# One queue's transfers laid out as landing in order, more zero groups, twelve pattern buffers in reused space

## The chip, the cores and the metric

The kernel runs on one core of a Trainium2 chip. The metric is the device time of one execution in microseconds (us). TensorE (PE) multiplies matrices into the eight PSUM banks; VectorE (DVE), ScalarE (ACT) and GpSimd (POOL) compute; SyncE (SP) issues almost all DMA transfers of this kernel, on one queue. Every engine runs its own instruction list in order and waits on semaphores for the others.

## The reference

One transformer layer in its parallel form, batch 1, 2048 rows of width 640, bf16: an attention with 32 query heads of 20 columns that share one key and one value head, and a feed-forward part with a squared ReLU (640 to 1536 to 640). Both read the same normalised input and both are added to it:

```python
def _A_ref(x, wq, wk, wv, wo):
    q = (x @ wq).reshape(B, S, 32, 20).transpose(0, 2, 1, 3)
    k = x @ wk
    v = x @ wv
    scores = jnp.einsum("bhqd,bkd->bhqk", q, k) * (20 ** -0.5)
    p = softmax(scores)
    o = jnp.einsum("bhqk,bkd->bhqd", p, v)
    return o.transpose(0, 2, 1, 3).reshape(B, S, 640) @ wo

def _B_ref(x, w1, b1, w2, b2):
    h = x @ w1 + b1
    r = jnp.where(h > 0, h, 0)
    return (r * r) @ w2 + b2

xn = layernorm(x)
out = x + _A_ref(xn, ...) + _B_ref(xn, ...)
```

## The kernel before, in words

**Tiling.** Queries come in 4 chunks of 512 rows, heads in 8 groups of four; a chunk and a group are a *block*, 32 in all, worked off in order. Within a block the keys come in 16 tiles of 128. One *unit* is one head of one key tile: a score matmul of 128 keys by 512 queries that fills one PSUM bank. There are 32 x 16 x 4 = 2048 units; up to four score matmuls use the four row strips of the array at once and count as one batch.

**Two ways to the exponential.** ACT takes two or three neighbouring banks in one instruction and writes exp into the ring `PT` (L1328). To relieve ACT, some key tiles (all four heads of one) go another way: DVE turns scores into 16-bit integer patterns that, read as bf16, are a piecewise-linear power of two (L1425, one bank each), and from these 2048 columns it makes three shifted copies (L1446); part of the third copies is made by POOL in pieces (L1508). The four patterns are averaged with weighted values `vp` by the value product. Patterns lie in `pbx`, `NPB` buffers of four banks' width. [...]

**Value product and norm.** The value product (L1615) sums a block into one PSUM bank; a column of ones in the values gives the softmax's denominator. `norm(b)` then copies the bank to `Tn` (L1660, DVE), spreads the denominator over the partitions by a DMA (L1663, `dn`), takes the reciprocal (L1665, DVE), sends it to a row by a second DMA (L1668, `Rr`), spreads it by a third (L1671, `Rb`, 256 KB), and POOL multiplies (L1676). Four DMAs (L1721) then pack the result into `OTp`. The last three blocks use `norm_last`: DVE transposes, reciprocal, multiply into `T2`, transpose back (L1696 to L1708).

**The rest.** Query projections (`u_QP`: PE, DVE L888, and 20-row DMAs L906 into `qT`), the feed-forward part (`u_FFN`: PE L777, DVE L933, POOL L941) and the output products are *units of filler work* for PE between the score batches, each tied to a position in blocks (`U(at, ...)`). For the last chunk, the output rows 12 to 15 (of 128 each) are split: `u_P1` does feed-forward and the attention parts that are ready, and puts the sum into `part` with the residual (L1055); `u_PF` adds the remaining head tiles after the last block; `u_PX` does one row (NPX = 1) in one go, residual included through an identity matmul. The residual `xres` is loaded again row by row (`x_again`, L952), in four buffers.

**What sets the order.** A planner in Python, run when the kernel is built. It holds a duration for every instruction and a landing time for every DMA, keeps a clock for each engine, and picks the next instruction by earliest start and priority. The result is one fixed list per engine; the semaphores are derived from it. On the chip the lists run as laid out, whatever the real durations. `PLAN` holds thresholds for each half block (how early scores are issued ahead of ACT, `lead`; how much work DVE should have waiting, `hungw`, `dstarv`; how many banks are kept for filler, `miscr`; and so on). `dma(eng, name, fn, deps, land, issue)` lays a transfer out as occupying its queue for `issue` ns and landing `land` ns after its start. `S_FILL` adds groups of four matmuls with zero weights (L1544) that change nothing in the sums, where PE's load over the last `PE_FWIN` = 1500 ns, in columns, is not over a limit: `PE_FILL` up to position `FILLPOS` = 4 blocks, `PE_FILL2` behind it.

Of the kernel before, what the change touches and what calls it, by code (L numbers as in the profile page):

```python
# [14 lines left out]
HPG = 4  # L15
# [35 lines left out]
NPB = 10  # L51
PHQ = 2
PHP_F, PHP_E = 156.0, 0.836
OVER = 40.0
PHU = 5000.0
NQS = 6
NQP = 2
EVP = 2
# [93 lines left out]
)]  # L152
PAAT = 24.7
PAQ = ()
NPX = 1
PQAT = (7.0, 10.5)
PQSTEP = .3
XRP = 2.0
PASTEP = .12
TLAND = 3050.0  # L160
TDMA = 4
NLAST = 3
NTN = 3
DAL, DBL, DCL, NBL, QSL, XRL = 2800.0, 2400.0, 7600.0, 2300.0, 2700.0, 3600.0
CLTL = 9000.0
PVEND = 0.5
PTOL = 500.0
# [1752 lines left out]
```

## Time and profile before

| | us |
|---|---|
| median of three runs | 703.27 (703.08 to 704.89) |
| the profiled execution | 703.88 |
| its span, first to last instruction | 702.2 |
| busy: PE / DVE / ACT / POOL | 684.5 / 669.6 / 675.8 / 415.4 |

The granted TensorE clock is 0.993 of full speed in the mean. PE's busy time counts matmuls that overlap, so it says little of how full PE is. In lines of the profile, `out<-in` names the tiles written and read, `x8` a count of instructions, and what stands in brackets is the engine's idle time before the line and who ended it; `SPq` is the DMA-issuing queue of SP, `issue` a wait for nothing that the profile shows.

### The profile page before, as it was taken

The numbers are of one execution on the slowest core, as the hardware profiler recorded it, in microseconds if no ns is written. First come the engines' busy times: TensorE is split into PE (matmuls) and PEld (weight loads), VectorE is DVE, ScalarE is ACT, GpSimd is POOL, SyncE is SP. The second block draws the span as 40 slices with busy tenths as digits, with TensorE's granted clock in tenths as the row PEclk, the third lists the DMA queues.
The fourth block names the chain that finished last, engine by engine and source line by source line (L and its number), as shares of the span: only waits on it lengthen the run. The fifth ranks groups of instructions, "written<-read, shape, count | busy, mean of one in ns | idle before, by whom it ended". The sixth has DMA issues, their size and how long they took to land.

```text
span 702.2 us, 23386 instructions
## 1 busy us (share of the span) xinstructions
PE 684.5 (97%) x9882; PEld 220.0 (31%) x9882; DVE 669.6 (95%) x1161; ACT 675.8 (96%) x696; POOL 415.4 (59%) x687
## 2 busy tenths in 40 slices
PE   8899899899999999999999999999999999999997
PEld 4322222222223333332222333333222233333335
DVE  7988899999999999999999999999999999999983
ACT  6999799999999999999999999999999999999993
POOL 2256476676764666667666666666776666645500
PEclk9999899999999999999999999999999999999999
DMA  7722222111100111111110121010110101112001
GB/s 209 181 50 66 71 76 66 25 22 29 27 17 10 37 27 44 38 29 33 28 27 16 25 50 41 17 43 18 44 30 18 23 17 33 42 34 52 21 2 40
DMA packets 38658, 29.46 MB, mean 42 GB/s; under 512 B 20922, under 2 KB 34203, under 8 KB 38555
## 3 DMA queue, kind: packets, MB, share of 16 engines
q1 hardware_dynamic: 37899, 27.95, 16.7%
q8 instruction: 79, 1.29, 0.8%
q14 instruction: 24, 0.20, 0.1%
q10 hardware_dynamic: 656, 0.03, 0.1%
HBM read 10.87 MB, written 2.62 MB: 19 GB/s over the span
## 4 chain that ended last, share of the span: by engine, by line
PE 48%; DVE 30%; ACT 16%; DMA 4%; issue 1%; SPq 1%; POOL 1%; DVEq 0%; POOLq 0%
PE ps L1615 17%; ACT PT L1328 16%; DVE pbx L1425 16%; PE ps L1148 15%; PE ps L777 15%; DVE pbx L1446 8%; DVE hT_tmp L933 2%; DMA Rb<-Rr 1%; DVE Tn L1660 1%; DMA dn<-Tn 1%; SPq L906 1%; DVE qpk L888 1%; DMA xnT<-big 1%; DVE stats L679 1%; DMA pbx<-in_A_x_dram 0%
## 5 line engine op out<-in xcount | busy, mean ns | idle before, releaser
L1328 ACT ACTIVATE PT<-ps 128x1024 bf16<-128x1024 f32 (+1 forms) x678 | 668.8, 1119 | 9.1 <-PE ps L1148 8.4
L1508 POOL TENSOR_SCALAR pbx<-pbx 128x576 int16<-128x576 uint16 (+15 forms) x509 | 311.5, 634 | 163.7 <-DVE pbx L1446 161.5
L1425 DVE TENSOR_SCALAR pbx<-ps 128x512 int16<-128x512 f32 (+1 forms) x583 | 381.7, 684 | 10.2 <-PE ps L1148 9.3
L1148 PE MATMUL ps<-qT,kT 20*128 20x512 bf16 x2048 | 265.6, 386 | 6.1 <-DVE hT_tmp L933 2.5
L1446 DVE TENSOR_SCALAR pbx<-pbx 128x2048 int16<-128x2048 int16 x313 | 214.4, 707 | 0.5
L1615 PE MATMUL ps<-pbx,vp 128*32 128x512 bf16 x1776 | 164.8, 387 | 2.7 <-DVE pbx L1446 1.4
L1148 PEld LDWEIGHTS ps<-qT,kT 20*128 20x128 bf16 x2048 | 66.3, 91 | 263.1 <-ACT PT L1328 159.9
L1615 PE MATMUL ps<-PT,vx 128*32 128x512 bf16 x1456 | 141.6, 384 | 1.6 <-ACT PT L1328 1.5
L777 PE MATMUL ps<-w_sb,big 128*32 128x320 bf16 x1536 | 80.0, 302 | 0.0
L777 PE MATMUL ps<-xnT,w_sb 128*32 128x512 bf16 x960 | 78.1, 388 | 0.0
L941 POOL TENSOR_TENSOR big<-hT_tmp 128x224 bf16<-128x224 bf16 (+5 forms) x90 | 56.9, 643 | 29.4 <-DVE pbx L1446 26.5
L1615 PEld LDWEIGHTS ps<-pbx,vp 128*32 128x32 bf16 x1776 | 42.6, 95 | 57.2 <-issue 39.6
L1615 PE MATMUL ps<-pbx,vx 128*32 128x512 bf16 x592 | 58.2, 386 | 0.7 <-DVE pbx L1425 0.6
L1615 PEld LDWEIGHTS ps<-PT,vx 128*32 128x32 bf16 x1456 | 37.4, 95 | 42.2 <-issue 31.9
L1676 POOL TENSOR_TENSOR OTs<-Tn,Rb 128x224 bf16<-128x224 f32 (+4 forms) x42 | 32.8, 782 | 28.3 <-DVE pbx L1446 26.1
L777 PEld LDWEIGHTS ps<-w_sb,big 128*32 128x32 bf16 x1536 | 31.9, 95 | 30.8 <-issue 23.6
L933 DVE TENSOR_SCALAR hT_tmp<-ps,b1col 128x512 bf16<-128x512 f32 x48 | 35.1, 731 | 0.6 <-PE ps L777 0.5
L777 PE MATMUL ps<-wo_p,OTp 120*32 120x320 bf16 (+1 forms) x640 | 33.5, 302 | 0.3 <-DVE pbx L1425 0.3
L777 PE MATMUL ps<-xnT,wq_sb 128*32 128x512 bf16 (+2 forms) x435 | 33.1, 373 | 0.0
L777 PEld LDWEIGHTS ps<-xnT,w_sb 128*32 128x32 bf16 x960 | 20.0, 95 | 26.9 <-issue 17.7
L1615 PEld LDWEIGHTS ps<-pbx,vx 128*32 128x32 bf16 x592 | 15.4, 95 | 18.8 <-issue 11.8
L1660 DVE COPY Tn<-ps 128x512 f32<-128x512 f32 x29 | 19.6, 676 | 0.2 <-PE ps L1615 0.2
(72 smaller groups left out, 172.3 us busy)
## 6 DMA issues: line engine op xcount, KB each, us to landing
Rb<-Rr SPq DMA_DIRECT2D x29, 256.0 KB
xres<-in_A_x_dram SPq DMA_DIRECT2D x16, 160.0 KB
out_dram<-out_sb SPq DMA_DIRECT2D x16, 160.0 KB
qT<-qpk SPq DMA_DIRECT2D x105, 20.0 KB
pbx<-in_A_x_dram SPq DMA_DIRECT2D x3, 640.0 KB
w_sb<-in_B_w_dram SPq DMA_DIRECT2D x1, 1920.0 KB
w_sb<-in_B_w_dram SPq DMA_DIRECT2D x4, 480.0 KB
OTp<-OTs SPq DMA_DIRECT2D x96, 20.0 KB
```

What stands on the lines that cost most here:

```text
L679: v = yield Req(("dve", 400.0, 470.0, [lambda e, hh=hh: e.bn_stats(out=stats6[:, st, hh, :], in_=x_sb[:, st, 320 * hh:320 * hh + 320])]), ...
L777: return lambda e: e.matmul(ps[32 * j:32 * j + m, b_[0], 0:n], Lj, R, start=first, stop=last, tile_position=(0, 32 * j))
L933: v = yield Req(("dve", 658.0, 742.0, [lambda e: e.tensor_scalar(out=hT_tmp[:, k, :], in0=ps[:, b_[0], :], scalar1=b1col[:, f:f + 1], scal ...
L941: w = yield from pieces(512, 139.0, 1.7, lambda c0, c1: (lambda e: e.tensor_tensor(out=h2T[:, qc % 2, f, c0:c1], in0=hT_tmp[:, k, c0:c1], ...
L1148: ins.append(lambda e, i=i, b=b, t=t, h=h: e.matmul(ps[:, i, :], kT[32 * h:32 * h + DH, t * 128:(t + 1) * 128], qT[32 * h:32 * h + DH, b % ...
L1328: op = yield Req(("act", d_, d_ + 107.0, [lambda e, slot=slot, n=n, src=src: e.activation(out=PT[:, slot:slot + n, :], in_=ps[:, src, :], ...
L1425: return Req(("dve", d_, d_ + 82.0, [lambda e: e.tensor_scalar(out=PB[:, k, hsl, :], in0=ps[:, bk:bk + np_, :], scalar1=OFFS, scalar2=0.0, ...
L1446: return Req(("dve", 600.0, 684.0, [lambda e: e.tensor_scalar(out=PB[:, k, :, :], in0=PB[:, s, :, :], scalar1=PH_D[j], scalar2=None, op0=A ...
L1508: return lambda e: e.tensor_scalar(out=PB[:, k, :, :].rearrange("p h n -> p (h n)")[:, c0:c1], in0=PBU[:, s, :, :].rearrange("p h n -> p ( ...
L1615: ins = [(lambda e, h=h, first=first, last=last: e.matmul(ps[32 * h:32 * h + 32, bk, :], lhs, rhs[h], start=first, stop=last, tile_positio ...
L1660: v = yield Req(("dve", 600.0, 682.0, [lambda e: e.tensor_copy(out=Tn[:, tb, :], in_=ps[:, pvb, :])]), (lambda: None if oldt() is None els ...
L1676: w = yield from pieces(512, 138.0, 2.14, lambda c0, c1: (lambda e: e.tensor_tensor(out=dst[:, c0:c1], in0=Tn[:, tb, c0:c1], in1=Rb[:, a, ...
```

## The change

The planner gets new rules and numbers, and some tiles move. The instructions stay the same in kind; their order changes from the third score batch on.

- A transfer that SP issues lands, in the plan, at least `QNEXT` = 100 ns after the one issued before it.
- The loads of `wo` and `b2` get issue times of 500, 370 and 300 ns (they stood at 60) and landing times of 5000 and 4000 ns (16000). The landing of `Rb` goes from 7600 to 7000 ns, the issue of an `xres` load from 650 to 500 ns.
- `PE_FILL2` goes from 1000 to 1400. A zero group reads `xnT` in place of `kT`.
- `NPB` goes from 10 to 12 buffers. Room comes from `xres` with three row buffers (`NXR`) in place of four, and from tiles put into others: the layernorm's statistics and `b1row` into `xres`, `Rr` into rows of `kT` that no product reads, `T2` into `wq_sb`, `ones_bf` into `OT7`. Waits that follow: the first two writes of `Rr` wait for all of `kT`; the first loads of `xres` wait for all normalised rows and for `b1`; the multiplies into `T2` wait for the last query projection.
- The row that `u_PX` does is 15 in place of 12; `u_P1` does 12 to 14.
- All 64 rows of `PLAN` are other numbers.

```diff
-NPB = 10
+NPB = 12
+NXR = 3
 PLAN = [...
-    (680.0, 3500.0, 600.0, 6000.0, 300.0, 900.0, 12, 2, 0.0, 3, 60.0, 300.0, 4.0),
...
+    (650.0, 3500.0, 600.0, 6000.0, 300.0, 900.0, 12, 2, 0.3, 3, 60.0, 300.0, 4.0),
...
-DAL, DBL, DCL, NBL, QSL, XRL = 2800.0, 2400.0, 7600.0, 2300.0, 2700.0, 3600.0
+DAL, DBL, DCL, NBL, QSL, XRL = 2800.0, 2400.0, 7000.0, 2300.0, 2700.0, 3600.0
+QNEXT = 100.0
-PE_FILL2 = 1000.0
+PE_FILL2 = 1400.0
+        self.queue = 0.0
             op.done = est + max(dur, lat) + (PESW if eng == "pe" and rr.mode != self.mode else 0.0)
+            if eng == "sp" and lat > dur:
+                op.done = self.queue = max(op.done, self.queue + QNEXT)
-        xres = sb("xres", [128, 4, D], BF16)
+        xres = sb("xres", [128, NXR, D], BF16)
+        xrow = xres[:, :, :].rearrange("p s d -> p (s d)")
+        stats6 = xrow[:, 0:384].bitcast(F32).rearrange("p (st h k) -> p st h k", st=ST, h=2)
...
+        b1row = xrow[0:FT, 544:672]
+        Rr = kT[:, 0:1024].bitcast(F32)
+        T2 = wq_sb[:, :, :].rearrange("p t n -> p (t n)")[:, 0:1024].rearrange("p (a n) -> p a n", a=2)
+        ones_bf = OT7[:, 0, 0:128]
-            dma("sp", f"xr{st}", lambda e: e.dma_start(xres[:, st % 4, :], xv[:, st, :]), [xuse[(st - 4, hh)] for hh in range(2)] if st >= 4 else [], XRL, 650.0)
+            dma("sp", f"xr{st}", lambda e: e.dma_start(xres[:, st % NXR, :], xv[:, st, :]), [xuse[(st - NXR, hh)] for hh in range(2)] if st >= NXR else [done[f"X{i}"] for i in range(ST)] + [done["B1"]], XRL, 500.0)
-            dma("sp", "wop", lambda e: e.dma_start(wo_p[0:HT * DH, 0:full, :], ...), [v], 16000.0)
+            dma("sp", "wop", lambda e: e.dma_start(wo_p[0:HT * DH, 0:full, :], ...), [v], 5000.0, 500.0)
-                dma("sp", f"wo{i}", lambda e, dst=dst, h=h: e.dma_start(dst, A_wo[h * DH:h * DH + DH, :]), [v], 16000.0)
+                dma("sp", f"wo{i}", lambda e, dst=dst, h=h: e.dma_start(dst, A_wo[h * DH:h * DH + DH, :]), [v], 4000.0, 370.0)
-                return [... e.matmul(ps[32 * h:32 * h + 32, pvb, :], zeros32[:, :], kT[:, 0:512], start=False, stop=False, ...) ...]
+                return [... e.matmul(ps[32 * h:32 * h + 32, pvb, :], zeros32[:, :], xnT[:, 0, 0:512], start=False, stop=False, ...) ...]
-            dma("sp", f"db{b}", lambda e: e.dma_start(Rr[a:128:32, :]..., rd[:, a, :]),
-                [w] + ([] if b < 2 else [done[f"dc{b - 2}"]]), DBL, 650.0)
+            dma("sp", f"db{b}", lambda e: e.dma_start(Rr[DH + a:128:32, :]..., rd[:, a, :]),
+                [w] + ([done[k] for k in ("K0a", "K0", "K1a", "K1", "K2", "K3")] if b < 2 else [done[f"dc{b - 2}"]]), DBL, 650.0)
-            st, hh = 4 * q3 + NPX + k // 2, k % 2
+            st, hh = 4 * q3 + k // 2, k % 2
         def S_PX(k):
-            st, hh = 4 * q3 + k // 2, k % 2
+            st, hh = ST - NPX + k // 2, k % 2
```

More of the change, by code (lines that the diff above doesn't have):

```diff
@@ L890, in u_QP @@
             rel(b_, v)
+            qlast.append(v)
             qpres[k].last = None
@@ L1012, in u_OUT @@
             done[f"O{qc}_{st}_{hh}"] = v
-            yield from out_tail(v, st, hh, xres[:, st % 4, cs], b_, [done[f"xr{st}"]])
+            yield from out_tail(v, st, hh, xres[:, st % NXR, cs], b_, [done[f"xr{st}"]])
         ptiles = {}
@@ L1020, in u_PA @@
             v = yield from groups(g_ffn2(qc, st, cs), 320, b_, w2_ops(), 4, f"PA_{st}_{hh}", gdeps=[[done[f"H{qc}_{f}"]] for f in range(FT)])
-            v = yield Req(("dve", 398.0, 483.0, [lambda e: e.tensor_tensor(out=part[:, st % 4, cs], in0=ps[:, b_[0], 0:320], in1=xres[:, st % 4, cs], op=ALU.add)]),
+            v = yield Req(("dve", 398.0, 483.0, [lambda e: e.tensor_tensor(out=part[:, st % 4, cs], in0=ps[:, b_[0], 0:320], in1=xres[:, st % NXR, cs], op=ALU.add)]),
                           [v, done[f"xr{st}"]] + [done[f"HR{QC - 1}_{f}"] for f in range(FT)], EVP, f"PE1_{st}_{hh}")
@@ L1031, in u_PQ @@
             done[f"HD{qc}_{st}_{hh}"] = v
-            v = yield Req(("dve", 398.0, 483.0, [lambda e: e.tensor_tensor(out=xres[:, st % 4, cs], in0=ps[:, b_[0], 0:320], in1=xres[:, st % 4, cs], op=ALU.add)]),
+            v = yield Req(("dve", 398.0, 483.0, [lambda e: e.tensor_tensor(out=xres[:, st % NXR, cs], in0=ps[:, b_[0], 0:320], in1=xres[:, st % NXR, cs], op=ALU.add)]),
                           [v, done[f"xr{st}"]], EVP, f"PE1_{st}_{hh}")
@@ L1043, in u_PB @@
             done[f"O{qc}_{st}_{hh}"] = v
-            yield from out_tail(v, st, hh, part[:, st % 4, cs] if qc == QC - 2 else xres[:, st % 4, cs], b_, [done[f"PP{st}_{hh}"]])
+            yield from out_tail(v, st, hh, part[:, st % 4, cs] if qc == QC - 2 else xres[:, st % NXR, cs], b_, [done[f"PP{st}_{hh}"]])
         def u_P1(st, hh, b_):
@@ L1054, in u_P1 @@
             v = yield from groups(g_wo(qc, st, cs, ts) + g_ffn2(qc, st, cs), 320, b_, w2_ops() + wo_ops(), 4, f"P1_{st}_{hh}", gdeps=n3 + n2)
-            v = yield Req(("dve", 450.0, 491.0, [lambda e: e.tensor_tensor(out=part[:, st % 4, cs], in0=ps[:, b_[0], 0:320], in1=xres[:, st % 4, cs], op=ALU.add)]), [v, done[f"xr{st}"], olast[(st - 4, hh)]], EVP, f"PE1_{st}_{hh}")
+            v = yield Req(("dve", 450.0, 491.0, [lambda e: e.tensor_tensor(out=part[:, st % 4, cs], in0=ps[:, b_[0], 0:320], in1=xres[:, st % NXR, cs], op=ALU.add)]), [v, done[f"xr{st}"], olast[(st - 4, hh)]], EVP, f"PE1_{st}_{hh}")
             done[f"PP{st}_{hh}"] = v
@@ L1069, in u_PX @@
             cs = half(hh)
-            gl = [((lambda j: ident[:, 32 * j:32 * j + 32]), xres[:, st % 4, cs])] + g_ffn2(qc, st, cs) + g_wo(qc, st, cs, range(NOT + 1))
+            gl = [((lambda j: ident[:, 32 * j:32 * j + 32]), xres[:, st % NXR, cs])] + g_ffn2(qc, st, cs) + g_wo(qc, st, cs, range(NOT + 1))
             gd = [lambda: get(f"xr{st}")] + [(lambda f=f: get(f"H{qc}_{f}")) for f in range(FT)] + [(lambda t=t: get(*tiles_of(qc, t, st))) for t in range(NOT + 1)]
@@ L1543, in fill @@
             def fill(pvb):
-                return [(lambda e, h=h: e.matmul(ps[32 * h:32 * h + 32, pvb, :], zeros32[:, :], kT[:, 0:512], start=False, stop=False, tile_position=(0, 32 * h))) for h in range(HPG)]
+                return [(lambda e, h=h: e.matmul(ps[32 * h:32 * h + 32, pvb, :], zeros32[:, :], xnT[:, 0, 0:512], start=False, stop=False, tile_position=(0, 32 * h))) for h in range(HPG)]
             prefill = [(lambda e, h=h: e.matmul(ps[32 * h:32 * h + 32, PVB, :], ones_bf[:, 0:32], hT_tmp[:, 0, :], start=True, stop=True, tile_position=(0, 32 * h))) for h in range(HPG)]
@@ L1556, in poll @@
                         return None
-                    return Req(("pe", PE512, PE512 + PELAT, fill(pvbank[max(pvbank)])), [done["zeros"], done["K0"]], 50, "fill", mode="col", cols=512.0, after=t + 40.0)
+                    return Req(("pe", PE512, PE512 + PELAT, fill(pvbank[max(pvbank)])), [done["zeros"]] + te4(0), 50, "fill", mode="col", cols=512.0, after=t + 40.0)
                 op = yield poll
@@ L1609, in poll @@
                         if it[0] == "A":
-                            rhs = {h: PT[:, s, :] for h, s, _ in it[2]}
-                            lhs = vx[:, it[1], :]
-                        else:
-                            rhs = {h: PB[:, it[2][1], h, :].bitcast(BF16) for h in range(HPG)}
-                            lhs = vp[:, it[1], it[2][0], :] if it[2][0] >= 0 else vx[:, it[1], :]
-                        ins = [(lambda e, h=h, first=first, last=last: e.matmul(ps[32 * h:32 * h + 32, bk, :], lhs, rhs[h], start=first, stop=last, tile_position=(0, 32 * h))) for h in range(HPG)]
+                            slot_of = {h: s for h, s, _ in it[2]}
+                            rhs = lambda h: PT[:, slot_of[h], :]
+                        else:
+                            rhs = lambda h: PB[:, it[2][1], h, :].bitcast(BF16)
+                        lhs = vp[:, it[1], it[2][0], :] if it[0] == "D" and it[2][0] >= 0 else vx[:, it[1], :]
+                        ins = [(lambda e, h=h, first=first, last=last: e.matmul(ps[32 * h:32 * h + 32, bk, :], lhs, rhs(h), start=first, stop=last, tile_position=(0, 32 * h))) for h in range(HPG)]
                         return Req(("pe", PE512, PE512 + PELAT, ins), dd + (bank[bk].last if first else []), (PVEND if cur_a[0] == NSB else PVU if sum(slot_busy) >= plan("ringhi") else 1) if b == min(pvbank, default=b) else 1.1, "PV", mode="col", cols=512.0)
@@ L1834, in S_PX @@
         def S_PX(k):
-            st, hh = 4 * q3 + k // 2, k % 2
-            yield Until(lambda: (pos() >= PXAT[k] and have(*[f"PP{st}_{hh}" for st in range(4 * q3 + NPX, ST) for hh in range(2)]) or "QKend" in done) and have(f"xr{st}") and have(*[f"H{q3}_{f}" for f in range(FT)]))
+            st, hh = ST - NPX + k // 2, k % 2
+            yield Until(lambda: (pos() >= PXAT[k] and have(*[f"PP{st}_{hh}" for st in range(4 * q3, ST - NPX) for hh in range(2)]) or "QKend" in done) and have(f"xr{st}") and have(*[f"H{q3}_{f}" for f in range(FT)]))
             hb = Hold([None])
@@ L1848, in g @@
                 yield from u_PF(st, hh, Hold([None]))
-            for st in range(4 * q3 + NPX, ST):
+            for st in range(4 * q3, ST - NPX):
                 for hh in range(2):
```

26 lines of the change are left out of this document (11 added, 15 removed), and 123 rows, old and new, of the table PLAN.

## The prediction

> **What bounds the kernel now.** First the page's totals and its chain.
>
> ```profile
> span 702.2 us, 23386 instructions
> PE 684.5 (97%) x9882; PEld 220.0 (31%) x9882; DVE 669.6 (95%) x1161; ACT 675.8 (96%) x696; POOL 415.4 (59%) x687
> PE 48%; DVE 30%; ACT 16%; DMA 4%; issue 1%; SPq 1%; POOL 1%; DVEq 0%; POOLq 0%
> ```
>
> Three engines are above 95%, and the chain changes between them, so the totals do not tell which one sets the pace. The list of waits does:
>
> ```profile
> PEld ps L1148 <- ACT PT L1328: 159.9, 414, 0.8
> ACT PT L1328 <- PE ps L1148: 8.4, 10, 2.6
> DVE rd L1665 <- DMA dn<-Tn: 2.7, 1, 2.7
> POOL OTs L1676 <- DMA Rb<-Rr: 2.2, 1, 2.2
> ```
>
> PE's score batches wait 414 times for ACT to free a bank, ACT only 10 times for scores. ACT is the bound, and the time is its busy time plus its idle time, 702.2 - 675.8 = 26.4 us. Where that lies, stages of 20 us show (columns: engine busy times in the order PE, PEld, DVE, ACT, POOL; then granted clock, DMA share, GB/s):
>
> ```profile
> 0.00:20.00 20.00, 17.32 (x222) 7.92 (x222) 15.34 (x50) 13.76 (x21) 5.13 (x23) 1.00 0.70 198
> 60.00:80.00 20.00, 17.46 (x205) 4.63 (x202) 15.30 (x27) 15.33 (x16) 10.40 (x15) 0.83 0.35 86
> 120.00:140.00 20.00, 18.16 (x240) 5.03 (x232) 18.94 (x30) 18.84 (x20) 12.81 (x20) 1.00 0.17 36
> 200.00:220.00 20.00, 18.70 (x242) 5.35 (x240) 18.73 (x32) 18.80 (x20) 11.06 (x19) 0.91 0.09 17
> 680.00:700.00 20.00, 18.35 (x433) 10.81 (x430) 9.44 (x23) 10.54 (x8) 0.00 (x0) 1.00 0.06 20
> ```
>
> ACT idles 6.24 in the start, 4.67, 1.16 and 1.20 in three stages, 11.66 behind its last exponential (680 + 10.54 to 702.2). That is 24.9 of the 26.4. So the questions are: do the three stalls go, does the tail shrink, does anything new come.
>
> **The change part by part.** *In-order landing (A).* The first stall, in the queue's order, then the chain and the engines:
>
> ```profile
> 63.77 0.57 SPq L1671 DMA_DIRECT2D Rb<-Rr  x1
> 65.62 0.54 SPq L1663 DMA_DIRECT2D dn<-Tn  x1
> 66.20 2.17 SPq L616 DMA_DIRECT2D w_sb<-in_B_w_dram  x1
> ```
>
> ```profile
> 65.62 5.75 DMA dn<-Tn
> ...
> 125.82 6.95 DMA Rb<-Rr
> ```
>
> ```profile
> 71.39 0.25 DVE L1665 RECIPROCAL rd<-dn 128x16 f32<-128x16 f32 x1 [2.70 <-DMA dn<-Tn]
> ...
> 72.93 1.02 ACT L1328 ACTIVATE PT<-ps 128x1024 bf16<-128x1024 f32 x1 [2.60 <-PE ps L1148]
> ```
>
> A small transfer is issued behind a 256 KB one and lands after 5.75 us. The big one, if it took 6.95 like the other that the chain shows, landed at 70.72, and the small one at 71.37. DVE stands at the reciprocal, its pattern work waits behind it, PE gets no bank, ACT idles 2.60. It does not end there (stages of 2 us, same columns):
>
> ```profile
> 70.00:72.00 2.00, 0.00 (x0) 0.00 (x0) 0.61 (x2) 0.33 (x1) 0.00 (x0) 0.78 0.72 200
> ...
> 74.00:76.00 2.00, 2.00 (x18) 0.38 (x20) 0.73 (x3) 1.06 (x2) 0.67 (x1) 0.50 0.16 33
> ...
> 204.00:206.00 2.00, 1.52 (x19) 0.52 (x19) 2.00 (x4) 2.00 (x3) 1.36 (x4) 1.00 0.24 49
> 206.00:208.00 2.00, 1.51 (x21) 0.43 (x19) 2.00 (x4) 2.00 (x3) 1.14 (x3) 0.91 0.23 47
> 208.00:210.00 2.00, 2.00 (x23) 0.41 (x15) 2.00 (x4) 1.73 (x2) 1.03 (x2) 0.50 0.00 0
> ```
>
> PE's granted clock falls to half, and PE then cannot feed ACT: the other 2.07 of the 4.67. In the changed list the second `dn` transfer stands ahead of the first `Rb`, so it has nothing long in front of it; `Rb` goes back by the 0.54 of that issue, with POOL's multiply laid out behind it. I take 4.6 off. Bounds: 0, if another reciprocal takes its place, and 4.67.
>
> *Issue times of the `wo` loads (B).* The second stall:
>
> ```profile
> 120.24 3.67 SPq L906 DMA_DIRECT2D qT<-qpk  x5
> 123.95 0.61 SPq L1668 DMA_DIRECT2D Rr<-rd  x1
> ```
>
> ```profile
> 132.91 1.27 POOL L1676 TENSOR_TENSOR OTs<-Tn,Rb 128x512 bf16<-128x512 f32 x1 [2.19 <-DMA Rb<-Rr]
> ...
> 137.48 3.41 ACT L1328 ACTIVATE PT<-ps 128x1024 bf16<-128x1024 f32 x3 [1.14 <-PE ps L1148]
> ```
>
> The block's `Rr` transfer is issued only when SP is through with ten `wo` loads and five 20-row transfers; `Rb` follows, POOL waits 2.19 for it, its pattern pieces queue behind, the value product waits for them, ACT loses 1.14. The changed list has `Rr` directly behind the `wo` loads, then the five, then `Rb`: `Rr` is issued 3.67 earlier and can land while the five are issued, so `Rb` goes out at about 120.24 + 0.61 + 3.67 = 124.5 in place of 125.82, 1.3 earlier; the five go 0.61 later, for blocks that are not yet at work. That alone covers 1.3 of POOL's 2.19; the rest is that the plan held 10 x 60 = 600 ns for these loads and now holds 3760, so that POOL's multiply stands where its input is there. I take 1.1 off; bounds 0 and 1.16.
>
> *Zero groups (C).* The third stall has no late transfer: from 204 to 208 PE has little to do (no filler unit lies there), the clock halves at 208, ACT loses 1.20.
>
> ```profile
> L1544 PE MATMUL ps<-kT,zeros 128*32 128x512 bf16 x64 | 4.9, 383 | 0.0
> ```
>
> 64 zero matmuls become 100; before, none stands behind score unit 60, after, 32 stand between units 439 and 559, and the low place was at unit 553. Counting columns issued per ten units, the lowest place before has 1584 and the next 2256 (no fall there); the lowest after has 2176. I take 1.2 off, bounds 0 and 1.20. The 36 cost 36 x 4.9 / 64 = 2.8 us of PE at most, in places where PE waits for ACT (159.9 us of that in all): nothing; up to 2.8 if the cover were gone. [...]
>
> *Batches.* Scores per way are equal (1456 units to ACT, 592 to DVE). ACT gets 551 pairs and 118 triples in place of 578 and 100:
>
> ```profile
> L1328 ACT ACTIVATE PT<-ps 128x1024 bf16<-128x1024 f32 (+1 forms) x678 | 668.8, 1119 | 9.1 <-PE ps L1148 8.4
> ...
> L1328 ACT ACTIVATE PT<-ps 128x1024 bf16<-128x1024 f32 x578 | 546.3, 1052 | 8.6 <-PE ps L1148 7.9
> L1328 ACT ACTIVATE PT<-ps 128x1536 bf16<-128x1536 f32 x100 | 147.7, 1506 | 0.5 <-PE ps L1148 0.5
> 679.54 11.00 ACT L1328 ACTIVATE PT<-ps 128x1536 bf16<-128x1536 f32 x8
> ```
>
> By the means, 27 x 1.052 - 18 x 1.506 = 1.3. They overlap, though: a triple takes (11.00 - 1.506) / 7 = 1.356 of ACT, and the page's 668.8 for both forms leaves (668.8 - 135.6) / 578 = 0.922 for a pair, so 24.9 - 24.4 = 0.5. I take 0.5 (bounds 0.5 and 1.3).
>
> *Twelve buffers.* DVE makes 316 shifted copies in place of 313:
>
> ```profile
> L1446 DVE TENSOR_SCALAR pbx<-pbx 128x2048 int16<-128x2048 int16 x313 | 214.4, 707 | 0.5
> ```
>
> At most 3 x 0.707 = 2.1 us; DVE idles 32.6 us in all, so nothing, and 2.1 if DVE were the bound. The tiles put into others add waits only early (`kT`, statistics, `b1` are long done when `Rr` and `xres` are first written) or for projections that end blocks earlier: nothing. With three `xres` buffers, row 15 loads only after both halves of row 12, and PE's first `u_PX` matmul has scores queued behind it. Eight score batches stand between, over 8 x 0.92 = 7.4 us; a load as slow as the slowest transfer shown, 6.95, is still hidden. If it were not, its excess would fall on ACT in full.
>
> *Tail (D).* Behind ACT's end at 690.54:
>
> ```profile
> 690.60 0.40 PE L1615 MATMUL ps<-PT,vx 128*32 128x512 bf16 x4
> 691.05 0.78 DVE L1696 STREAM_TRANSPOSE Tn<-ps 128x256 f32<-128x256 f32 x2 [2.54 <-PE ps L1615]
> 693.27 0.31 PE L777 MATMUL ps<-wo,OT 128*32 128x320 bf16 x4
> 695.04 1.80 PE L777 MATMUL ps<-w_sb,big 128*32 128x320 bf16 x48
> 697.45 2.48 DVE L991 TENSOR_TENSOR out_sb<-ps,w_sb 128x320 bf16<-128x320 f32 x6
> 697.63 0.72 PE L777 MATMUL ps<-wo,OT 128*32 128x320 bf16 x16
> ```
>
> A group of four takes (1.80 - 0.31) / 11 = 0.135. From the first `wo,OT` group on, 36 groups stand in the list before, 17 in the list after: the 48 feed-forward matmuls of one `u_P1` half are now in front, where PE waits for ACT. PE would end 19 x 0.135 = 2.6 earlier, at 695.8. Seven evacuations on DVE (the eighth is now ACT's), 0.40 apart, can start at about 693.9 and end at 696.8, where 699.93 is now; the output transfers behind them stay 2.27. That is 3.1; PE alone gives 2.6, and six pattern copies now stand just ahead of DVE's transposes. I take 3.0, bounds 2.0 and 3.4.
>
> *What comes new.* A new order has its own late transfers, which no row of before shows. Bounds: 0, and 7.0, as much as the old three (4.67 + 1.16 + 1.20). I take 1.5, near the two small stalls, because each of the old ones has its cause in the list of edits.
>
> Sum: -4.6 - 1.1 - 1.2 - 0.5 - 3.0 + 1.5 = -8.9. Against the profiled execution's 703.88 that is 695.0; that execution lies 0.61 above the median, so for the median 703.27 I say **694.4**, with 691 to 698 as this case's own range.
>
> **The rivals.**
> 1. *New waits cost what the old ones did.* -10.4 + 7.0 gives 699.9. For: all blocks keep a reciprocal behind a DMA. Against: outside three stages the old order lost nearly nothing.
> 2. *Slower: `Rb` lands later than laid out.* Its landing is now planned at 7.0 us where the chain shows 6.95, so no room is left, and POOL waits as at 132.91, 1.14 us of ACT each. To be slower by over 0.3% it has to eat 10.4 + 2.1, that is 11 of 29 blocks; with 17 of them, 703.3 - 10.4 + 19.4 = 712. For: the old figure, 7.6, left 0.65 of room. Against: even then the one wait came from a late issue, and a late piece of POOL has cover mostly.
> 3. *Transfers don't land in order.* Then the 5.75 us came from the weight load issued at 66.20, which moved 200 GB/s beside it, and the wait stays: 694.4 + 4.6 = 699.0. Against: it landed 0.65 behind the big one. [...] No run here has yet shown a later transfer landing first.
> 4. *It does nothing:* the stalls go and come back elsewhere and the tail's gain is spent; within 0.3% of 703.3.
>
> **How the numbers follow.** About 0.3%, 2.1 us, is what a measurement can tell from no change. Chances: forecast 0.58 (0.1 of it for zero groups that do not keep the clock up, 694.4 + 1.2 = 695.6, inside its range), rival 1 0.17, rival 3 0.04, rival 4 0.04, rival 2 0.17. Faster is 0.58 + 0.17 + 0.04 = 0.79, the same 0.04, slower 0.17. The low end takes all terms at their bounds with nothing new, 4.67 + 1.16 + 1.20 + 1.3 + 3.4 = 11.7 (691.6), less 1.6 for the 26.4 - 24.9 = 1.5 us of idle time not named above: 690. The high end, 703, takes in rivals 1, 3 and most of 4 and leaves out rival 2.
>
> **What would show it.** Right: no stage behind 40 us with ACT under 19.5 of 20; no wait of a reciprocal for `dn`; clock 1.00 from 60 to 220; zero groups between 140 and 210 us; 9 us or less from ACT's last exponential to the end. Wrong: DVE or POOL lines with a DMA as releaser, a clock at 0.50 at any place, or PE waiting for `xres` near the end.

## The result, and the profile after

The changed kernel takes 693.69 us (median of four executions, 693.49 to 693.96) against 703.92 (703.08 to 704.89) for the kernel before on the same chip: ratio 0.9854, 95% interval 0.9837 to 0.9872. Forecast were 694.4, with 691 to 698 as the narrower and 690 to 703 as the wider range. In the experiments below a few executions took 8 to 19 us longer than the others of their kernel at a lower clock (one was profiled, and stands at half clock from 25 to 73 us); they are left out, except that three in the run with both queue moves and one each in the runs without the queue's rule and with ten buffers are in the medians given there. The profiled execution took 693.49 with a span of 691.7 and a mean granted clock of 0.999. Line numbers are now those of the changed kernel, 6 to 8 higher than before in the same functions.

The page's totals and the engines of its chain:

```profile
span 691.7 us, 23430 instructions
PE 677.9 (98%) x9918; PEld 220.5 (32%) x9918; DVE 671.0 (97%) x1166; ACT 675.6 (98%) x688; POOL 411.1 (59%) x688
PE 56%; ACT 23%; DVE 20%; issue 1%; DMA 0%; DVEq 0%
```

ACT is busy for the same time as before to 0.2 us (675.8 there), and the span is 10.5 shorter. So nearly all that was gained is idle time of ACT: 26.4 before, 691.7 - 675.6 = 16.1 now. The list of waits (engine and line, what it waited for: us, times, longest):

```profile
PEld ps L1156 <- ACT PT L1336: 163.9, 428, 1.0
DVE Tn L1704 <- PE ps L1623: 4.4, 1, 4.4
ACT PT L1336 <- PE ps L1156: 1.6, 3, 0.6
POOL OTs L1684 <- DMA Rb<-kT: 1.6, 1, 1.6
```

The reciprocal's 2.7 behind `dn` is gone. POOL has one wait for `Rb` left, and ACT three for scores, 1.6 in all against 8.4. Stages of 20 us (columns as before: PE, PEld, DVE, ACT, POOL, then clock, DMA share, GB/s) show where:

```profile
0.00:20.00 20.00, 16.89 (x215) 7.66 (x219) 15.54 (x51) 13.83 (x22) 5.12 (x23) 1.00 0.71 199
20.00:40.00 20.00, 18.68 (x277) 6.26 (x273) 18.95 (x42) 19.37 (x25) 8.04 (x15) 1.00 0.82 177
40.00:60.00 20.00, 19.73 (x265) 5.59 (x262) 17.49 (x29) 19.44 (x22) 11.44 (x19) 1.00 0.06 15
60.00:80.00 20.00, 19.88 (x254) 5.26 (x253) 19.95 (x35) 20.00 (x22) 13.43 (x22) 1.00 0.37 96
120.00:140.00 20.00, 19.45 (x268) 5.67 (x260) 20.00 (x35) 19.88 (x21) 12.74 (x20) 1.00 0.14 30
200.00:220.00 20.00, 19.40 (x307) 6.68 (x299) 19.03 (x33) 19.94 (x19) 10.80 (x17) 1.00 0.07 14
```

ACT's idle time is 0.00, 0.12 and 0.06 in the three stages that lost 4.67, 1.16 and 1.20. The clock is 1.00 in all of them. Only 20 to 60 us shows anything else, 0.63 + 0.56; in the kernel before these two stages were

```profile
20.00:40.00 20.00, 17.97 (x268) 6.19 (x264) 19.03 (x43) 19.11 (x25) 7.09 (x14) 1.00 0.78 177
40.00:60.00 20.00, 20.00 (x269) 5.63 (x261) 17.70 (x30) 19.93 (x22) 12.46 (x18) 1.00 0.07 16
```

with 0.89 + 0.07.

SP's queue around the first stall, in order of time:

```profile
64.63 0.56 SPq L1671 DMA_DIRECT2D dn<-Tn  x1
65.24 0.54 SPq L1679 DMA_DIRECT2D Rb<-kT  x1
65.82 0.48 SPq L622 DMA_DIRECT2D w_sb<-in_B_w_dram  x1
67.89 0.57 SPq L1676 DMA_DIRECT2D kT<-rd  x1
74.14 0.54 SPq L1679 DMA_DIRECT2D Rb<-kT  x1
```

`dn` stands ahead of the 256 KB transfer. The transfer that carries its reciprocal away (`kT<-rd`, which is `Rr`) is issued 3.26 behind it, so `dn` landed in less than that; behind the big one it took 5.75. The slow landing is not gone from the queue, it has moved to `Rr`: the next `Rb`, which reads it, is issued 6.25 behind it (67.89 to 74.14), where that took 1.84 before (71.67 to 73.51). No engine waits for it there.

The last part, in order of time (start, length, engine, operation):

```profile
675.04 8.16 ACT L1336 ACTIVATE PT<-ps 128x1536 bf16<-128x1536 f32 x6
683.26 0.40 PE L1623 MATMUL ps<-PT,vx 128*32 128x512 bf16 x4
683.71 0.78 DVE L1704 STREAM_TRANSPOSE Tn<-ps 128x256 f32<-128x256 f32 x2 [4.41 <-PE ps L1623]
686.08 0.58 PE L783 MATMUL ps<-wo,OT 128*32 128x320 bf16 x12
687.25 2.25 DVE L999 TENSOR_TENSOR out_sb<-ps,w_sb 128x320 bf16<-128x320 f32 x5
688.12 0.44 PE L783 MATMUL ps<-wo,OT 128*32 128x320 bf16 x8
```

ACT ends at 675.04 + 8.16 = 683.20 and the span 8.5 later, where it was 11.66. From the first `wo,OT` group PE needs 2.48 (686.08 to 688.56) in place of 5.08 (693.27 to 698.35).

### The profile page after: what moved, and what is told of

Its sections match the earlier page's. It is cut to its first block, busy times and chain, and to the rows that moved or that the text cites. A ratio compares the mean times of both kernels' runs of the same rounds, so it can differ in the third digit from the quotient of the medians.

```text
span 691.7 us, 23430 instructions
## 1 busy us (share of the span) xinstructions
PE 677.9 (98%) x9918; PEld 220.5 (32%) x9918; DVE 671.0 (97%) x1166; ACT 675.6 (98%) x688; POOL 411.1 (59%) x688
## 4 chain that ended last, share of the span: by engine, by line
PE 56%; ACT 23%; DVE 20%; issue 1%; DMA 0%; DVEq 0%
ACT PT L1336 23%; PE ps L1623 20%; PE ps L1156 18%; PE ps L783 17%; DVE pbx L1433 11%; DVE pbx L1454 5%; DVE hT_tmp L941 2%; DVE Tn L1668 1%; DMA pbx<-in_A_x_dram 0%; DVE xres L685 0%; PE ps L1552 0%; DVE qpk L895 0%; PE ps L842 0%; DVE rd L1673 0%; DVE out_sb L999 0%
## 5 line engine op out<-in xcount | busy, mean ns | idle before, releaser
L1516 POOL TENSOR_SCALAR pbx<-pbx 128x576 int16<-128x576 uint16 (+15 forms) x506 | 306.6, 627 | 182.1 <-DVE pbx L1454 180.4
L1156 PE MATMUL ps<-qT,kT 20*128 20x512 bf16 x2048 | 261.5, 384 | 4.9 <-DVE pbx L1433 2.3
L1623 PE MATMUL ps<-pbx,vp 128*32 128x512 bf16 x1776 | 161.6, 383 | 0.3 <-DVE pbx L1454 0.3
L949 POOL TENSOR_TENSOR big<-hT_tmp 128x288 bf16<-128x288 bf16 (+5 forms) x95 | 57.3, 618 | 19.6 <-DVE pbx L1454 19.4
```

Of the source, the lines that this page charges most:

```text
L949: w = yield from pieces(512, 139.0, 1.7, lambda c0, c1: (lambda e: e.tensor_tensor(out=h2T[:, qc % 2, f, c0:c1], in0=hT_tmp[:, k, c0:c1], ...
L1156: ins.append(lambda e, i=i, b=b, t=t, h=h: e.matmul(ps[:, i, :], kT[32 * h:32 * h + DH, t * 128:(t + 1) * 128], qT[32 * h:32 * h + DH, b % ...
L1516: return lambda e: e.tensor_scalar(out=PB[:, k, :, :].rearrange("p h n -> p (h n)")[:, c0:c1], in0=PBU[:, s, :, :].rearrange("p h n -> p ( ...
L1623: ins = [(lambda e, h=h, first=first, last=last: e.matmul(ps[32 * h:32 * h + 32, bk, :], lhs, rhs(h), start=first, stop=last, tile_positio ...
```

## The experiments

The runs were taken on several chips. The kernel before has a median of 703.25 to 703.92 on them, so a difference of two medians from different chips is good to about 0.7 us. Ratios are to the kernel before on the same chip.

### The queue's order alone

Two runs take the kernel before, with its plan as it was, and move entries in SP's list only. The first puts the block's second `dn` ahead of the first `Rb`, directly ahead of it and of the weight load:

```diff
+        # SP's finished list: the first Rb ("dc0") goes behind the second dn
+        move("dc0", "w20")     # to the place ahead of the weight load
```

> The kernel before, its lists as they were, but on SP alone the first broadcast into Rb is issued behind the second dn transfer (they change places). No other engine's list changes. In-order theory (term A): the dn transfer lands about 2 to 3 us after its issue in place of 5.75, the 2.70 us wait of the reciprocal and the half clock behind it go, ACT's busy time from 60 to 80 us rises from 15.33 to over 19, and the time falls by 4 to 4.7 us, to about 699.3. Rival 3 (the weight load beside it made it slow): the dn transfer still takes over 5 us, the wait stays near 2.7 and the time stays within 1 us of 703.9. A third way: the stall only moves, because Rb goes out 2.4 us later and POOL waits for it; then a POOL wait on Rb of about 1 to 2 us appears and less than half of the 4.6 is won.

Measured: 699.32 against 703.86, ratio 0.9912 (0.9888 to 0.9936), 4.5 us less. Its queue and the stage:

```profile
67.31 0.57 SPq L1663 DMA_DIRECT2D dn<-Tn  x1
67.92 0.54 SPq L1671 DMA_DIRECT2D Rb<-Rr  x1
68.51 0.48 SPq L616 DMA_DIRECT2D w_sb<-in_B_w_dram  x1
70.57 0.57 SPq L1668 DMA_DIRECT2D Rr<-rd  x1
```

```profile
20.00:40.00 20.00, 17.82 (x243) 5.81 (x240) 17.53 (x41) 17.52 (x23) 6.24 (x13) 0.91 0.76 177
60.00:80.00 20.00, 19.78 (x274) 5.76 (x271) 19.95 (x34) 20.00 (x21) 13.82 (x19) 1.00 0.32 79
```

The weight load still follows 1.20 behind `dn`, and `dn` is done within 3.26. So the weight load was not what held it; the transfer ahead of it was. Term A stands: the stage's 4.67 is gone. The 4.5 of the medians holds more than that, though. In this profile the dip of the clock near 208 us is gone as well (1.20), and another has come at 32 us (the first line; 17.52 of ACT where the kernel before has 19.11), both in stretches whose lists are as before. The one execution with a clock of 1.000 took 698.01.

The third rival as it was priced, the weight load, falls. That transfers of this queue land in order is still no rule, by the traces' records of landings (up to sixteen for a transfer here): in the changed kernel an `Rr` issued at 299.55 had landed by 301.67, and the last of the sixteen parts of an `xres` row issued ahead of it, at 299.08, came at 303.11. The profile before already holds such a pair: the load of `b2`, issued at 119.94, had landed by 122.55, the `wo` load ahead of it, issued at 119.57, by 123.18. What the runs show is narrower. `dn` took 1.89 us in the median of its 29 transfers, in the kernel before and in the changed one, and behind an `Rb` 5.75 us in the kernel before and 6.11 in the run with the second move below; its reciprocal waited 2.7 us for it in the kernel before, 2.9 and 3.1 in the runs below with zero groups alone and with the second move alone, and with `dn` ahead of `Rb`, in this run and in the changed kernel, that wait is gone. In the changed kernel twelve of the sixteen parts of the weight load issued at 65.82 landed by 69.77, ahead of the last part of the `Rb` issued before it, at 65.24 (72.65), and four behind that, by 73.94.

The second move puts the five 20-row transfers near 120 us behind both `Rr` and `Rb`:

```diff
+        for n in ("Q6_3", "Q7_3"):      # the five qT transfers
+            move(n, "NB3")              # to a place behind the block's Rb
```

> The kernel before with the five 20-row transfers into qT near 120 us moved behind the block's Rr and Rb on SP; no other list changes. Issue-time theory (term B): Rr goes out at about 120.2 and Rb at about 122.1, lands near 129, before POOL's multiply at 130.7; POOL's 2.19 us wait and ACT's 1.14 us go, the stage from 120 to 140 us shows ACT at 19.9 or more, the time falls by 1.0 to 1.2 us, to about 702.8. Rival: the wait of PE for POOL's pattern piece has another cause (POOL is simply behind); then POOL's wait goes, PE's wait of about 1.2 us at 136.7 stays, and the time does not move by more than 0.3 us.

Measured: 701.86, ratio 0.9958 (0.9939 to 0.9977), 2.0 us less. POOL's wait for `Rb` is gone and ACT is full in the stage:

```profile
120.00:140.00 20.00, 19.41 (x254) 5.35 (x246) 19.97 (x33) 20.00 (x20) 12.95 (x22) 1.00 0.22 47
200.00:220.00 20.00, 18.70 (x270) 5.92 (x266) 20.00 (x34) 20.00 (x21) 11.41 (x20) 1.00 0.09 19
```

The first line is term B, 1.16 of idle time gone. The second line was not expected: the dip of the clock near 208 us is gone too, though there every list is the same as before and only starts 0.4 us earlier (the same gap of PE, 0.49 us long, stands at 205.81 in place of 206.25). The two stages gain 2.4 in the profile; the medians differ by 2.0. The wait that the forecast put at 1.0 to 1.2 is 1.16 of this, and the rest goes with the clock. Whether the new issue times are what made the planner choose the new order was not tested.

### Zero groups put in by hand

The kernel before with groups of zero matmuls between score units 521 and 569, each behind a group of the value product, two to a score batch at most. The trace shows 84 matmuls, which is 21 groups, and not the 17 (68 matmuls) that the expectation names:

```diff
+        # behind a value-product group: four matmuls with zero weights into the same bank
+        if 520 <= units_ < 572 and left_ and o in pv_bank: at_.append(o)
```

> The kernel before with 17 zero groups (68 matmuls of zero weights, the sums stay as they are) put into PE's list between score units 521 and 569, about 195 to 210 us; nothing else changes. Activity theory (term C): the granted clock stays at 1.00 from 200 to 220 us, ACT's busy time there rises from 18.80 to 19.9 and the time falls by about 1.2 us, to 702.7. [...] Third way: the groups stand in the way of scores, PE keeps its clock but ACT waits for scores; then ACT's waits for PE from 200 to 210 us stay at 1 us or more.

Measured: 706.25, ratio 1.0029 (1.0013 to 1.0044): slower. The stage, and ACT's instructions in it (in brackets idle time and releaser):

```profile
200.00:220.00 20.00, 18.94 (x266) 5.72 (x262) 17.64 (x29) 18.39 (x19) 10.86 (x19) 1.00 0.08 15
```

```profile
196.97 6.37 ACT L1328 ACTIVATE PT<-ps 128x1024 bf16<-128x1024 f32 x6 [0.49 <-PE ps L1148]
...
207.66 4.60 ACT L1328 ACTIVATE PT<-ps 128x1024 bf16<-128x1024 f32 x4 [0.40 <-PE ps L1148]
212.76 7.46 ACT L1328 ACTIVATE PT<-ps 128x1024 bf16<-128x1024 f32 x8 [0.49 <-PE ps L1148]
```

The clock keeps 1.00, and ACT loses 1.61, more than the dip's 1.20, and another 0.90 in the stage before (19.10 of 20 from 180 to 200 us, where the kernel before has 20.00). This is the third way of the expectation: the groups stand ahead of scores that ACT waits for. The same groups with both queue moves:

```diff
+        move("dc0", "w20")
+        for n in ("Q6_3", "Q7_3"):
+            move(n, "NB3")
         # and the zero groups as above
```

> The kernel before with all three of these at once, otherwise its own lists. Theory: the three terms are independent and add, 4.6 + 1.1 + 1.2 = 6.9 us, 697.0; the tail (11.66 us behind ACT's last exponential) stays as it was, so the rest to the changed kernel's 693.7 is the tail's 3.2. Rival (waits only move): less than half of it, over 700.5.

Measured: 699.95, ratio 0.9925 (0.9899 to 0.9951), the clock at 1.00, and ACT at 18.57 and 18.92 of 20 in 180 to 200 and 200 to 220 us. That is 3 us above the theory and just under the rival's 700.5: both moves keep their worth, the groups do not bring theirs. The two moves without the groups (the three lines above alone):

> The kernel before with both moves on SP's queue (the block's dn ahead of Rb, Rr ahead of the five 20-row transfers) and no zero group. If the two terms add up and the half clock near 208 comes and goes with the time at which the stretch is reached: 703.9 - 4.6 - 2.0 = 697.3, clock 1.00 from 80 to 220, two to three us below the run with the zero groups put in by hand (699.95). If the zero groups were what kept the clock up in that run: clock 0.50 near 200 and about 698.5.

Measured: 697.81, ratio 0.9937 (0.9902 to 0.9972). Its ten executions differ by more than others here. Four had a mean clock of 0.999 or 1.000 and took 696.12 to 696.61, two 0.997 or 0.998 and took 697.75 and 697.87, and three 0.985 and took 704.44 to 704.73; without these three the median is 696.61. The profiled one, 699.15 at 0.995, shows the dip (and the one at 32 us, ACT at 17.54 in 20 to 40 us):

```profile
200.00:220.00 20.00, 19.04 (x254) 5.78 (x258) 18.68 (x32) 18.77 (x20) 10.62 (x18) 0.91 0.07 16
```

So one list dips in some executions and not in others. That the forecast of 697.3 came so near to 697.81 is in part luck: the median lies between executions with a dip and executions without. The waits themselves add up: ACT is at 20.00 in 60 to 80 and in 120 to 140 us, and the executions without a dip, 696.4 against 703.25 for the kernel before on this chip, gain 6.9, where the three stages had lost 4.67 + 1.16 + 1.20 = 7.0. The groups by hand keep the clock up and cost 699.95 - 696.4 = 3.5 us against the executions without a dip; 0.6 of this can be the other chip.

### The changed kernel without its late zero groups

The 32 zero matmuls behind score unit 100 are left out (they add zeros); nothing else moves.

```diff
+            if o.name == "fill" and units_ > 100:
+                o.ins = []
```

> The changed kernel without the 32 zero matmuls that stand behind score unit 100 (160.8 to 199.5 us); nothing else moves in any list. Three outcomes are told apart. (i) The groups keep the clock up, as term C has it: a stage between 160 and 220 us shows a granted clock under 1.00 and ACT loses about 1.2 there, 694.9 in all against 693.7. (ii) The half clock near 208 of before was a matter of where a low stretch fell in time, as the three runs of before with a moved list suggest (clock 1.00 there with no zero group): 693.7, ACT idle in 160 to 220 as in the changed kernel. (iii) The groups cost something, as the ones put in by hand did: up to 32 x 4.9 / 64 = 2.5 us less, 691.2 to 693.5, with ACT's idle time in 160 to 220 below the changed kernel's.

Two of its four executions took 693.81 and 694.01; only they are compared. Once more, with more executions:

> The changed kernel without its 32 late zero matmuls once more, in more executions, because the dip near 208 us came in some executions of one list and not in others (with both queue moves and no zero group, 200 to 220 us showed a clock of 0.91 in one execution while four others kept 0.999 or 1.000 over the whole span). If the zero groups keep the clock up: a good part of the executions show a mean clock of 0.996 to 0.998 and 1 to 2 us more. If the changed kernel's order is full enough by itself: all stand at 0.999 or 1.000 and the time stays at 693.7 to 694.0.

Measured: 693.62 (693.59 to 694.71). Three of four executions stand at 693.6 with a clock of 1.000, one at 694.71 with 0.997. The profile of the changed kernel for 180 to 200 us, then the one without the groups for 180 to 220 us:

```profile
180.00:200.00 20.00, 18.60 (x255) 5.37 (x251) 20.00 (x34) 20.00 (x20) 13.55 (x23) 1.00 0.11 23
```

```profile
180.00:200.00 20.00, 18.06 (x235) 5.10 (x231) 20.00 (x34) 20.00 (x20) 13.54 (x23) 1.00 0.11 23
200.00:220.00 20.00, 19.40 (x307) 6.67 (x299) 19.02 (x33) 19.94 (x19) 10.84 (x17) 1.00 0.07 14
```

The groups fill 0.54 of PE in places where ACT is at 20.00 with them and without. They cost nothing, and in five of the six executions compared they save nothing; one of six took 1.1 more at a clock of 0.997, the size of one dip. Where in that execution the clock fell was not recorded.

### The last part

The changed kernel with row 12 in place of row 15 held back for the end, as before:

```diff
-            st, hh = ST - NPX + k // 2, k % 2
+            st, hh = 4 * q3 + k // 2, k % 2
```

> The changed kernel with row 12 in place of row 15 held back for the end, as before had it; only the lists of the last part differ. Behind the last value product PE's list has 76 groups in place of 36, and 58 in place of 17 from the first wo,OT group on. If the tail is PE's groups, as term D has it: 41 x 0.135 = 5.5 us more behind ACT's end, 699.2, and the stages up to 660 us as they were. If the end is set by DVE's transposes and evacuations alone: within 1 us of 693.7.

Measured: 699.49, ratio 0.9936 (0.9911 to 0.9962), 5.8 more than the changed kernel; 5.5 was worked out from the 41 groups. In the profile ACT ends at 684.02 and the span 14.2 later, 5.6 more than the 8.5 of the changed kernel. PE runs without a gap from 682 to 694 us. Why the list has so much left for the end, the trace shows:

```profile
685.17 1.80 PE L783 MATMUL ps<-w_sb,big 128*32 128x320 bf16 x48
688.44 1.80 PE L783 MATMUL ps<-w_sb,big 128*32 128x320 bf16 x48
688.89 0.42 SPq L960 DMA_DIRECT2D xres<-in_A_x_dram  x1
690.75 1.80 PE L783 MATMUL ps<-w_sb,big 128*32 128x320 bf16 x48
691.24 0.49 DVE L1063 TENSOR_TENSOR w_sb<-ps,xres 128x320 f32<-128x320 f32 x1 [2.77 <-DMA xres<-in_A_x_dram]
```

With three `xres` buffers rows 12 and 15 share one (15 - 12 = 3). Row 12, held back, keeps it to the end; row 15 is loaded at 688.89, behind ACT's end, and its products and evacuations with it. So the row swap goes with the loss of the fourth `xres` buffer, and that with the twelve pattern buffers.

Two rows held back in place of one:

```diff
-NPX = 1
+NPX = 2
```

> The changed kernel with two rows in place of one held back for the end; only the last part differs. 48 groups stand behind the last value product in place of 36 and 27 in place of 17 from the first wo,OT group on, and PE has 12 groups less to do ahead of it. By the groups: 10 x 0.135 = 1.4 later, 695.1; if the room that it makes ahead of the last score is worth as much, 693.7 or less.

Measured: 695.47, 695.67 and 696.68, 2.0 more than the changed kernel in the middle one; 1.4 was worked out from ten groups. In the profile 10.3 us stand behind ACT's end in place of 8.5. The sign is that of the groups. No gain ahead of the last score came back: ACT ends at 684.05, where the changed kernel has 683.20.

### The change with one part undone

Each of these is planned anew, so all its lists differ. First the queue's rule left out:

```diff
             if eng == "sp" and lat > dur:
-                op.done = self.queue = max(op.done, self.queue + QNEXT)
+                pass
```

> The changed kernel with the in-order rule of the queue left out of the planner; everything is planned anew. Known from the lists: ACT gets 620 pairs, 77 triples and a single, 8.5 us more by 0.922 and 1.356 each; 25 groups in place of 17 from the first wo,OT group on, 1.1 more. Without a stall that is 703.3, with no reciprocal and no POOL line held by a DMA for over 1 us. If the rule is what kept late landings out: the waits for dn or Rb come back, 2 to 5 us of ACT's idle time in a stage between 60 and 140 us, 705 to 708.

Then ten pattern buffers, the rest as changed:

```diff
-NPB = 12
+NPB = 10
```

> The changed kernel with ten pattern buffers; planned anew. ACT gets 599 pairs, 91 triples and a single, 8.2 us more; 20 groups in place of 17 in the last part, 0.4 more. If ACT stays fed, 702.3, all of the loss in ACT's busy time and none in its idle time ahead of 680 us, which would say that the buffers are worth what they let the planner take off ACT. If fewer buffers also starve VectorE: ACT's or DVE's idle time ahead of 680 grows by several us and it ends above 704.

Then the 64 rows of thresholds of before under the new rules:

```diff
-    (650.0, 3500.0, 600.0, 6000.0, 300.0, 900.0, 12, 2, 0.3, 3, 60.0, 300.0, 4.0),
+    (680.0, 3500.0, 600.0, 6000.0, 300.0, 900.0, 12, 2, 0.0, 3, 60.0, 300.0, 4.0),
...
```

> The changed kernel with the thresholds of before; planned anew. ACT gets 574 pairs and 108 triples, 7.6 us more; the last part has 19 groups behind the last value product in place of 36, 1.2 less by the last eight wo,OT groups against 17. If the stalls stay away by the queue's rule alone: 693.7 + 7.6 - 1.2 = 700.1, with ACT at 19.5 or more in all stages from 60 to 640 us. If the new thresholds are what kept them away: a stage with ACT under 19 and 702 or more.

Measured: 707.93, 707.61 and 708.21, ratios to the kernel before 1.0057 (1.0039 to 1.0075), 1.0069 (1.0040 to 1.0097) and 1.0067 (1.0045 to 1.0090). All three are slower than the kernel before. In time each is the second way of its expectation, 4.6, 5.3 and 8.1 us above the first. The totals of the three, in that order:

```profile
PE 689.7 (98%) x9878; PEld 222.4 (31%) x9878; DVE 660.5 (94%) x1137; ACT 683.7 (97%) x716; POOL 399.3 (57%) x645
```

```profile
PE 686.6 (97%) x9858; PEld 222.0 (31%) x9858; DVE 660.0 (94%) x1129; ACT 683.9 (97%) x710; POOL 404.3 (57%) x656
```

```profile
PE 684.9 (97%) x9910; PEld 221.1 (31%) x9910; DVE 660.2 (93%) x1124; ACT 684.0 (97%) x701; POOL 396.9 (56%) x631
```

The 8.1 to 8.4 us more of ACT are about as worked out (8.5, 8.2 and 7.6): in each of these lists ACT has 1472 score units in place of 1456, and DVE, with 16 fewer, is busy for 660 in place of 671. The rest is mostly idle time of ACT ahead of the last part, 4.1, 4.4 and 6.5 us more than in the changed kernel. A reciprocal waits for `dn` only with ten buffers, once, for 1.0 us. Without the rule the stage of 200 to 220 us is the worst:

```profile
200.00:220.00 20.00, 19.79 (x267) 5.81 (x264) 16.88 (x27) 17.92 (x20) 13.88 (x17) 1.00 0.10 22
```

That is not the mechanism that its expectation gave: no DMA holds a line there, the clock is 1.00, and yet ACT loses 2.08; the chain in this stretch runs through DVE and POOL. The place of `dn` in the queue does not come from the rule alone either. Without the rule the second `dn` is still issued ahead of the first `Rb` (64.84 and 65.45). With the rule and the thresholds of before it is issued behind (67.47 and 65.76), the list has its reciprocal only at 73.89, and nothing waits; with the rule and ten buffers it is behind as well (69.04 and 66.61), and that is the wait of 1.0. With ten buffers the loss is early (ACT 17.80 and 18.25 of 20 in 20 to 60 us), and POOL waits three times for `Rb`, 4.4 us in all. With the old thresholds it is spread:

```profile
ACT PT L1336 <- PE ps L1156: 8.2, 19, 0.7
```

Which threshold fits which stretch was not taken apart, nor whether others would win the loss back. The tail of this last list is 8.1 us with 8 groups from the first `wo,OT` group on, only 0.5 less than the changed kernel's with 17, where its expectation took off 1.2.

## Why the prediction was right, and where it was not

The time came within 0.7 us and for the most part for the reasons named; in one term, zero groups, the number was right by luck. By the steps of the prediction:

- **ACT's idle time is the account.** Right. Idle time fell by 10.3 us, busy time by 0.2, the span by 10.5.
- **A, in-order landing, -4.6.** Right in mechanism and size for the move: 4.67 of idle time became 0.00, and the move alone gives 4.5, with two dips of the clock in the account. That the planner's in-order rule is what made the move is not shown: without the rule `dn` still stands ahead.
- **B, the `wo` issue times, -1.1.** Right in size (1.16 became 0.12). The step "that alone covers 1.3 of POOL's 2.19; the rest is that the plan held ..." was not tested: moving the five transfers in the old plan took the whole wait away without it, but there they went behind `Rb` too, and in the changed list `Rb` stands behind them.
- **C, zero groups, -1.2.** The saving came (1.20 became 0.06), but not from the groups, so the number was luck: without them the stage is the same in the profile and the median stays within 0.1. The failed step is the reading that the low stretch from 204 to 208 us (PE busy for 1.52 and 1.51 of 2 us) brings the half clock behind it. One list, that with both queue moves, gave the dip in its profiled execution (0.91 from 200 to 220 us) and a mean clock of 0.999 or 1.000 in four others, so a low stretch alone does not settle it (the last section has more). Why the changed order escapes it so often stays open. It is not that it has no low stretch: from 364 to 368 us the changed kernel has PE busy for 3.03 of 4 us, as much as the kernel before from 204 to 208, and a clock of 1.00, with the late groups, none of which lies there, and without them. The prediction's bound of 0 for this term was the true one for the groups.
- **Batches, -0.5.** Measured -0.3: 668.8 became

```profile
L1336 ACT ACTIVATE PT<-ps 128x1024 bf16<-128x1024 f32 (+1 forms) x669 | 668.5, 1139 | 2.5 <-PE ps L1156 1.6
```

- **Twelve buffers, 0.** The three more copies cost nothing, as said. With ten, under the new thresholds, ACT gets 16 units more and the time is 13.9 worse. The other two lists that were planned anew give ACT the same 16 units more, and the kernel before does with 1456 units on ten buffers, so what the buffers themselves are worth stays open.
- **D, the tail, -3.0.** Right: 11.66 became 8.5, and the two changes of the groups' number go the same way, 0.14 and 0.18 us for a group behind ACT's end (5.6 / 41 and 1.8 / 10) where 0.135 was used.
- **What comes new, +1.5.** The one term that was mis-sized. In the stages where something new could be seen, 20 to 60 us, ACT idles 1.19 against 0.96 before: 0.2, which is no more than executions of one list differ by there (with row 12 held back, and the same list in this stretch, it is 1.73). Measured against its own kernel before, the change gave 10.2 where 8.9 was forecast, and this term is the difference. Of the signs of being right that the prediction named, one is just missed: 40 to 60 us has ACT at 19.44, under 19.5. Of the signs of being wrong one shows, the POOL line that waits for `Rb`.

The rivals: new waits (1) cost 0.2 and not 7.0. `Rb` later than laid out (2) shows as one POOL wait of 1.6 that ACT does not feel; with ten buffers POOL waits for it three times, so the mechanism is there and lacks its cover only in a worse plan. No order in landing (3) fell with the first run as far as the weight load is meant; transfers do land out of order in these traces (the `Rr` of 299.55 by 301.67, the `xres` row of 299.08 by 303.11), only not at the first stall of the kernel before, where `Rb`, `dn` and the weight load were done in the order of their issue, at 71.14, 71.37 and 72.88.

## What to carry to other kernels

Where a small transfer on the path stands behind a large one of the same queue, move it ahead before looking at bandwidth: one moved entry was worth 4.5 us here, where the whole change gives 10.2. Count the groups that a list leaves behind the bound engine's last instruction; beyond 17 each was paid in full here (0.14 and 0.18 us a group), and a list with nine fewer ended only 0.5 us sooner behind that instruction. A plan's thresholds, its buffers and its model of the queue hang together: taken back singly, each of the three made this kernel slower than before the change, so a part's worth can't be read from a run with that part undone unless the rest is held fixed.

## What was not expected of the hardware

The fall of TensorE's clock to half is not settled by the instruction list. With 200 to 208 us unchanged in the list, the clock was 0.91 in that stage for the kernel before and 1.00 in the two runs with one queue move each; ten executions of the kernel with both moves had mean clocks from 0.985 to 1.000 and times from 696.12 to 704.73. The longest gap of PE there was 0.49 us in the kernel before and in the run with the second move.

The traces show more. In the profiles of the kernel before and of the changed kernel the changes of the clock stand whole multiples of 3.41 us apart (in the kernel before the first fall comes 64.85 us, 19 of them, after the first rise, and the next 129.71 us, 38 of them, after the clock is up again; in the changed kernel the one fall comes 686.08 us, 201 of them, after the rise). The first rise comes 6.27 us behind the first instruction in the one and 4.90 in the other. So the changes of a profile lie on a grid of 3.41 us, at another place in each of the two. Cut up by that grid, the same low stretch of PE lies in one window in the kernel before, and half clock follows; in the run with `dn` moved it is divided between two, and the clock stays:

```profile
204.25:207.66 3.41, 2.45 (x34) 0.74 (x30) 3.41 (x7) 3.41 (x5) 2.47 (x5) 1.00 0.25 50
207.66:211.07 3.41, 3.41 (x34) 0.64 (x26) 2.42 (x5) 2.32 (x2) 2.10 (x4) 0.50 0.02 4
```

```profile
199.52:202.93 3.41, 2.77 (x35) 0.84 (x31) 3.41 (x7) 3.41 (x4) 2.54 (x5) 1.00 0.24 49
202.93:206.34 3.41, 2.92 (x41) 0.84 (x37) 3.41 (x7) 3.41 (x4) 1.58 (x4) 1.00 0.13 28
```

PE's busy share of a window does not decide by itself, though: in the run with `dn` moved a window from 131.3 us on has PE busy for 0.61 and no fall behind it (the stage of 120 to 140 us has 1.00), and one from 28.9 us on has 0.82 and a fall (20 to 40 us, 0.91). What sets off a fall stays open. One dip cost about 1.1 us (694.71 at a mean clock of 0.997 against 693.6 at 1.000), and preventing it by hand cost more than that (699.95 - 696.4 = 3.5).
